# A fused transformer block: order of the LayerNorm statistics, choice of the tile transposed ahead of K, and the PSUM banks that go with them

## Chip, cores, metric

One core of one Trainium2 chip. The metric is device time in microseconds of one execution. The kernel before took 245.29 us (median of 3; 245.23 to 245.52). A program on one core has no sister core to compare with; by the rule used here a run more than 1.5% above the fastest of its kernel is slow.

## The reference, cut to what matters

```python
B, N, D = 2, 256, 1152          # 512 tokens: tiles 0,1 are batch 0, tiles 2,3 batch 1
mod = (_silu(c) @ w_mod).reshape(B, 6, 1, D)
shift_a, scale_a, gate_a, shift_m, scale_m, gate_m = [mod[:, i] for i in range(6)]
h = _layernorm(x) * (1 + scale_a) + shift_a
qkv = (h @ wqkv)...             # then attention, @ wo, a second LayerNorm, fc1, gelu, fc2
```

This is about the first 14 us: the first LayerNorm, the columns of `1 + scale_a`, and the start of the K projection.

## The kernel before

Every operation is a unit with its reads and writes; a scheduler orders the units (PE in program order, the head of VectorE by a list) and derives the waits. It tracks PSUM by bank and orders any two engines that touch one bank, one after the other (in the trace of before ScalarE's hk_2_0 starts at 12.13 us, VectorE's hk_1_0 on the same bank has ended at 12.09).

```python
for t in range(4):                       # statistics of LN1
    if t in (1, 2): ln_stats_dve(...)    # VectorE: 3 bn_stats (L743), aggregate (L744), + eps (L746); GpSimd: pow -0.5 (L747)
    else:           ln_stats_act(...)    # ScalarE: sum (L751), sum of squares (L753); then var (L754), GpSimd pow (L755)
    dve(... (x - m) * rs ..., "xn_%d" % t)                                   # L764

XB = [(4, 5, 3), (6, 5, 7)]              # PSUM banks of the transposed tiles, by batch
KB = [(0, 1, 2, 3), (4, 5, 6)]           # PSUM banks of K's accumulators, by batch
...                                      # warm(n): n matmuls 128x512 whose result nobody reads
xn_T(1)                                  # 9 transposes of tile 1 (L695)
warm(1, "c"); sca(0, 3)                  # 12 matmuls 128x2 for the scale columns; 1st w_mod load
xn_T(0)
warm(1, "d"); sca(3, 6)                  # 2nd w_mod load
warm(1, "e"); sca(6, 9)                  # 3rd w_mod load
hk(0, 0)                                 # VectorE: scale k-tile 0 of batch 0 (L809), reads the scales in PSUM
...                                      # ScalarE copies tiles 0 and 1 out of banks 5 and 3 (L687)
xn_T(3, 0, 8)                            # 8 transposes of tile 3
k_first(0); k_first(1)                   # K, k-tiles 0 and 1, batch 0: 16 matmuls 128x256
xn_T(3, 8, 9); xn_T(2)
```

## Time and profile before

| | before |
|---|---|
| time, median | 245.29 us |
| span of the profiled run | 243.3 us |
| PE busy | 98% |
| x first used (VectorE's first statistics) | 4.78 us |
| K's first 128x256 matmul | 11.78 us |
| last VectorE instruction (L1273) | starts 241.06 us |

### The profile page before, as it was taken

What the parts mean: (1) busy time and instruction counts of PE and PEld (TensorE: products, weight loads), DVE (VectorE), ACT (ScalarE), POOL (GpSimd) and SP (SyncE); (2) the same over time, 40 slices, a digit from 0 to 9 for tenths busy, and PEclk for the clock granted to TensorE, in tenths of its full rate; (3) what the DMA queues carried; (4) which work ended last, traced back from release to release, by engine and by line L of the source; (5) the groups of instructions that cost most, each with busy time, mean ns of one, the idle gap of its engine ahead of it and who ended that gap; (6) DMA issues with size and microseconds to landing.
All of it is one profiled execution on the core that took longest, in us unless ns stands there. A gap on an engine that the chain in (4) does not pass through costs nothing.

```text
span 243.3 us, 4087 instructions
## 1 busy us (share of the span) xinstructions
PE 238.9 (98%) x1763; PEld 148.1 (61%) x1763; DVE 120.4 (49%) x217; ACT 67.2 (28%) x136; POOL 21.4 (9%) x39
## 2 busy tenths in 40 slices
PE   7999999999999999999999999999999999999995
PEld 2698854556667666898444444444565666656575
DVE  3824378596997799789999500000022221111112
ACT  4830350345424207973233222223000000000000
POOL 1500000000021186400000000020000000000000
PEclk9999999999999999999999999999999999999999
DMA  7999999999995999989953498002000000000000
GB/s 233 332 379 393 390 390 391 396 414 405 392 354 183 341 396 392 392 268 394 316 160 84 150 320 310 0 21 80 0 16 19 16 16 19 16 16 22 29 16 19
DMA packets 30140, 51.59 MB, mean 212 GB/s; under 512 B 1703, under 2 KB 15787, under 8 KB 30123
## 3 DMA queue, kind: packets, MB, share of 16 engines
q1 hardware_dynamic: 29680, 50.14, 57.9%
q0 software_dynamic: 416, 1.19, 1.7%
q8 instruction: 14, 0.23, 0.4%
q14 instruction: 3, 0.02, 0.0%
q10 hardware_dynamic: 27, 0.00, 0.0%
HBM read 50.14 MB, written 1.19 MB: 211 GB/s over the span
## 4 chain that ended last, share of the span: by engine, by line
PE 94%; ACT 2%; DMA 2%; DVE 1%; POOL 0%; issue 0%; DVEq 0%
PE psum L692 93%; PE psum L695 2%; DMA arena<-in_x_dram 2%; ACT arena L753 1%; ACT arena L751 1%; DVE arena L764 0%; POOL arena L755 0%; DVE arena L1272 0%; DVE arena L1273 0%; DVE arena L754 0%; DVE arena L746 0%; DVEq L476 0%
## 5 line engine op out<-in xcount | busy, mean ns | idle before, releaser
L692 PE MATMUL psum<-arena 128*128 128x384 bf16 (+10 forms) x1674 | 235.7, 307 | 1.5 <-POOL arena L715 1.5
L692 PEld LDWEIGHTS psum<-arena 128*128 128x128 bf16 (+3 forms) x1674 | 142.9, 97 | 90.1 <-issue 4.5
L1067 DVE SCALAR_TENSOR_TENSOR arena<-arena 128x1152 f32<-128x1152 bf16 x32 | 44.7, 1414 | 0.6
L1272 DVE TENSOR_TENSOR arena<-psum,arena 128x384 f32<-128x384 f32 (+3 forms) x14 | 7.0, 501 | 68.0 <-PE psum L692 68.0
L1181 ACT ACTIVATE arena<-psum 128x512 bf16<-128x512 f32 (+1 forms) x44 | 22.4, 520 | 42.7 <-PE psum L692 42.7
L687 ACT ACTIVATE arena<-psum 128x512 bf16<-128x512 f32 (+6 forms) x37 | 19.6, 550 | 38.7 <-PE psum L692 37.0
L689 DVE CAST arena<-psum 128x512 bf16<-128x512 f32 (+3 forms) x13 | 8.2, 641 | 11.4 <-PE psum L692 11.3
L673 POOL DMA_DIRECT2D dit_scratch<-arena x3 | 1.8, 616 | 115.3 <-DVE arena L689 58.5
L1149 POOL TENSOR_TENSOR arena<-arena 128x384 f32<-128x384 f32 x12 | 10.9, 912 | 10.8 <-DVE arena L1148 9.4
L1094 DVE CAST arena<-psum 72x32 bf16<-72x32 f32 x1 | 0.2, 188 | 21.3 <-PE psum L692 21.3
L743 DVE BATCH_NORM_STATS2 arena<-arena 128x6 f32<-128x384 f32 (+1 forms) x18 | 9.6, 551 | 0.3
L1154 ACT ACTIVATE arena<-arena 128x1152 bf16<-128x1152 f32 x4 | 5.3, 1344 | 11.8 <-DVE arena L1153 11.8
L1273 DVE TENSOR_TENSOR arena<-arena 128x384 bf16<-128x384 f32 (+3 forms) x14 | 7.0, 501 | 0.5
L1148 DVE TENSOR_TENSOR arena<-psum,arena 128x384 f32<-128x384 f32 x12 | 6.5, 547 | 1.5 <-PE psum L692 1.4
L695 PE MATMUL psum<-arena 128*128 128x128 bf16 (+1 forms) x89 | 7.1, 219 | 0.2 <-DVE arena L764 0.2
L695 PEld LDWEIGHTS psum<-arena 128*128 128x128 bf16 (+1 forms) x89 | 5.8, 98 | 2.2 <-DMA arena<-in_c_dram 0.8
L1168 DVE TENSOR_SCALAR arena<-psum,arena 128x128 bf16<-128x128 bf16 x20 | 5.4, 334 | 1.9 <-PE psum L695 1.9
L1171 ACT ACTIVATE arena<-psum,arena 128x128 bf16<-128x128 bf16 x16 | 6.0, 456 | 1.0 <-PE psum L692 0.6
L1074 DVE TENSOR_REDUCE arena<-arena 128x36 f32<-128x1152 f32 x4 | 5.4, 1345 | 0.0
L1071 DVE STREAM_TRANSPOSE arena<-arena 128x1152 f32<-128x1152 f32 x4 | 5.4, 1362 | 0.0
L997 ACT ACTIVATE arena<-psum,arena 128x256 bf16<-128x256 f32 x8 | 3.7, 472 | 1.3 <-PE psum L692 0.9
L951 ACT ACTIVATE arena<-arena 128x256 bf16<-128x256 bf16 x6 | 2.6, 498 | 3.9 <-DVE arena L945 3.9
(48 smaller groups left out, 45.9 us busy)
## 6 DMA issues: line engine op xcount, KB each, us to landing
arena<-in_w_fc_dram SPq DMA_DIRECT2D x9, 1152.0 KB, 7.1
arena<-in_w_fc_dram SPq DMA_DIRECT2D x4, 2592.0 KB, 17.3
arena<-in_wqkv_dram SPq DMA_DIRECT2D x18, 288.0 KB, 10.4
arena<-in_w_mod_dram SPq DMA_DIRECT2D x3, 1728.0 KB, 20.3
arena<-in_w_mod_dram SPq DMA_DIRECT2D x3, 864.0 KB, 13.4
arena<-in_w_mod_dram SPq DMA_DIRECT2D x9, 288.0 KB, 10.7
arena<-in_wqkv_dram SPq DMA_DIRECT2D x1, 2592.0 KB, 16.7
arena<-in_wo_dram SPq DMA_DIRECT2D x1, 2592.0 KB, 24.4
```

Of the source, the lines that this page charges most:

```text
L687: act(c_act(n), lambda e: e.activation(out=dst, in_=src, func=ACTF.Copy), [src], [dst], name)
L689: dve(c_dve_psum16(n) if psum16 else c_dve_psum32(n), lambda e: e.tensor_copy(dst, src), [src], [dst], name)
L692: S.instr(lambda e: e.matmul(o, lhsT=l, rhs=r, start=st, stop=sp, **kw), reads=[l, r], writes=[o])
L695: S.instr(lambda e: e.transpose(o, i_, idn), reads=[i_, idn], writes=[o])
L743: dve(550, lambda e, s=s, o=o: e.bn_stats(out=o, in_=s), [s], [o], "bn_%s_%d" % (tag, ci))
L1067: dve(1270, lambda e, w=w, s=s, acc=acc: e.scalar_tensor_tensor(out=acc, in0=w, scalar=s, in1=acc, op0=ALU.mult, op1=ALU.add), [w, s, acc] ...
L1148: dve(550, lambda e, o=o, ga=ga, x1c=x1c: e.tensor_tensor(out=x1c, in0=o, in1=ga, op=ALU.mult), [o, ga], [x1c], "wo_t1_%d_%d" % (t, ci))
L1149: S.op("pool", 930, lambda e, xs=xs, x1c=x1c: e.tensor_tensor(out=x1c, in0=x1c, in1=xs, op=ALU.add), reads=[x1c, xs], writes=[x1c], name=" ...
L1171: act(440, lambda e, o=o, dst=dst, s1=s1, s2=s2: e.activation(out=dst, in_=o, func=ACTF.Identity, scale=s1, bias=s2), [o, s1, s2], [dst], ...
L1181: act(c_act(ntok), lambda e: e.activation(out=dst, in_=o, func=ACTF.Gelu_apprx_tanh), [o], [dst], "gelu_%d_%d" % (f, tok0))
L1272: dve(c_dve_psum32(w), lambda e, o=o, gm=gm, t1=t1: e.tensor_tensor(out=t1, in0=o, in1=gm, op=ALU.mult), [o, gm], [t1], "fc2_t1_%d_%d" % ( ...
L1273: dve(c_dve_32(w), lambda e, t1=t1, x1c=x1c, ost=ost: e.tensor_tensor(out=ost, in0=t1, in1=x1c, op=ALU.add), [t1, x1c], [ost], "fc2_out_%d ...
```

## The change

Its intent: the tile whose transposes stand ahead of K shall be one that does not wait for ScalarE's four passes over x. So tile 2 takes tile 3's place, its statistics run without xn_0 between them, tile 0 is transposed later, and banks are renamed so that tile 2's transposes and K find free ones.

```diff
-XB = [(4, 5, 3), (6, 5, 7)]
+XB = [(4, 5, 3), (6, 2, 7)]
-KB = [(0, 1, 2, 3), (4, 5, 6)]
+KB = [(0, 1, 5, 3), (4, 2, 6)]
 sca(0, 3)
-xn_T(0)
 warm(1, "d")
 sca(3, 6)
+xn_T(0)
...
-xn_T(3, 0, 8)
+xn_T(2, 0, 8)
...
-xn_T(3, 8, 9)
-xn_T(2)
+xn_T(2, 8, 9)
+xn_T(3)
 # VectorE's list
-"xn_1", "bn_ln1_2_1", "xn_0", "bn_ln1_2_2", "aggr_ln1_2", "var_ln1_3", "veps_ln1_2", "xn_3", "hk_0_0", ..., "xn_2"
+"xn_1", "bn_ln1_2_1", "bn_ln1_2_2", "aggr_ln1_2", "veps_ln1_2", "xn_0", "var_ln1_3", "xn_2", "hk_0_0", ..., "xn_3"
 # GpSimd
-S.order_after(by["rstd_ln1_2"], by["rstd_ln1_3"])
+S.order_after(by["rstd_ln1_3"], by["rstd_ln1_2"])
```

More of the change, by code (lines that the diff above doesn't have):

```diff
@@ L960, in build_kernel @@
             "dve": ["zq4b", "c_half", "c_silu", "bn_ln1_1_0", "bn_ln1_1_1", "bn_ln1_1_2", "aggr_ln1_1", "veps_ln1_1", "bn_ln1_2_0",
-                    "xn_1", "bn_ln1_2_1", "xn_0", "bn_ln1_2_2", "aggr_ln1_2", "var_ln1_3", "veps_ln1_2", "xn_3", "hk_0_0", "sc1a_0", "hk_1_0",
-                    "xn_2", "hk_0_1", "hk_1_1", "hk_2_1", "hk_3_1", "hk_%d_0" % KC, "sc1a_4", "hk_%d_1" % KC] + ["hk_%d_%d" % (kt, b) for kt in range(KC + 1, KT) for b in range(2)],
+                    "xn_1", "bn_ln1_2_1", "bn_ln1_2_2", "aggr_ln1_2", "veps_ln1_2", "xn_0", "var_ln1_3", "xn_2", "hk_0_0", "sc1a_0", "hk_1_0",
+                    "xn_3", "hk_0_1", "hk_1_1", "hk_2_1", "hk_3_1", "hk_%d_0" % KC, "sc1a_4", "hk_%d_1" % KC] + ["hk_%d_%d" % (kt, b) for kt in range(KC + 1, KT) for b in range(2)],
             "act": ["ld_c", "c_tanh", "sum_ln1_0", "sq_ln1_0", "sum_ln1_3", "sq_ln1_3", "xnT_cp0_4", "xnT_cp0_8", "hk_2_0", "hk_3_0",
```

## The prediction

K's start moves from 11.78 to 11.59 us, a gain of 0.19, shaded to 0.18, and 245.29 - 0.18 gives 245.11. "16 such matmuls" are K's 128x256 ones, and "serialises them by bank" speaks of two engines at one bank.

> **What bounds the kernel now.** I read the page first: busy shares, then the chain that ended last, then the costliest groups.
>
> ```profile
> span 243.3 us, 4087 instructions
> PE 238.9 (98%) x1763; PEld 148.1 (61%) x1763; DVE 120.4 (49%) x217; ACT 67.2 (28%) x136; POOL 21.4 (9%) x39
> PE 94%; ACT 2%; DMA 2%; DVE 1%; POOL 0%; issue 0%; DVEq 0%
> L692 PE MATMUL psum<-arena 128*128 128x384 bf16 (+10 forms) x1674 | 235.7, 307 | 1.5 <-POOL arena L715 1.5
> L695 PE MATMUL psum<-arena 128*128 128x128 bf16 (+1 forms) x89 | 7.1, 219 | 0.2 <-DVE arena L764 0.2
> ```
>
> TensorE (PE) holds 94% of the chain and stands idle for 1.5 us at the start and 0.2 us once later. The remaining 6% of the chain, some 14 us, is the head, and the chain in order of time shows it (columns: start, length, what).
>
> ```profile
> 8.50 1.26 ACT arena L753 x2
> ...
> 9.86 0.16 DVE arena L754
> 10.02 0.07 DVE arena L746
> ...
> 10.10 0.56 POOL arena L755
> 10.66 0.03 issue
> 10.69 0.59 DVE arena L764
> 11.28 0.05 issue
> 11.32 0.62 PE psum L695 x8
> 11.94 1.75 PE psum L692 x16
> 13.69 0.56 PE psum L695 x10
> 14.25 45.14 PE psum L692 x382
> ```
>
> Up to 11.32 us the chain is the LayerNorm of token tile 3: ScalarE sums its squares (L753), VectorE makes the variance (L754), GpSimd 1/sqrt (L755), VectorE normalises (L764), and PE transposes it. From 11.32 on nothing but PE is in the chain until the final eviction. So a change in the head is worth exactly the time by which PE's unbroken stream starts earlier, provided no new gap appears behind it. PE is called busy before 11.32 too, but much of that is warm-up matmuls whose result nobody reads, and a few real ones.
>
> The timeline of the last two microseconds before that stream shows who else stands close behind (start, length, engine, line, operation).
>
> ```profile
> 8.44 0.58 DVE L764 TENSOR_SCALAR arena<-arena 128x1152 bf16<-128x1152 bf16 x1
> 8.94 0.55 DVE L743 BATCH_NORM_STATS2 arena<-arena 128x6 f32<-128x384 bf16 x1
> 9.52 0.23 DVE L744 BATCH_NORM_AGGREGATE arena<-arena 128x2 f32<-128x18 f32 x1
> 10.00 1.30 ACT L687 ACTIVATE arena<-psum 128x1024 bf16<-128x1024 bf16 x2 [0.24 <-PE psum L695]
> 10.62 0.68 POOL L747 TENSOR_TENSOR arena<-arena 128x1 f32<-128x1 f32 x1
> 10.68 0.38 PEld L692 LDWEIGHTS psum<-arena 128*128 128x128 bf16 x12 [0.28 <-DMA arena<-in_w_mod_dram]
> 11.28 0.35 DVE L809 TENSOR_SCALAR arena<-psum 128x256 bf16<-128x256 bf16 x1
> 11.32 0.45 PEld L695 LDWEIGHTS psum<-arena 128*128 128x128 bf16 x8 [0.26 <-DVE arena L764]
> ```
>
> The line to see is 10.68: the last twelve scale matmuls (`sca(6,9)`) waited 0.28 us for the third load of w_mod. They end at about 11.15 by the trace. So the removed wait (xn_3 at 11.28) has a second limiter only some 0.2 us ahead of it.
>
> [...] `k_first(0)` and `k_first(1)`, 16 such matmuls, run from 11.78 to 13.53, 109 ns each. [...] I expect no clock effect. [...] The kernel serialises them by bank, and the trace agrees: ScalarE's hk_2_0 starts at 12.13, just after VectorE's hk_1_0 on the same bank ends at 12.09. That is why the diff renames banks. [...]
>
> **The change part by part.** No instruction is added or removed; the order changes on PE, VectorE and GpSimd only. All times are estimates from the durations above.
>
> VectorE: the second and third stats pieces of tile 2 run back to back (7.91, then 8.40 at the 0.49 us spacing that tile 1's three showed: 1.48/3), to 8.95. Aggregate 8.98 to 9.22, add epsilon 9.25 to 9.40, then xn_0 at 9.32 to 9.90 instead of 8.44 to 9.02: 0.88 us later. The small variance operation of tile 3 follows at about 9.86 to 10.02. GpSimd takes tile 2's 1/sqrt at 9.43, some 0.57 us, to 10.00. xn_2 then runs from 10.05 to 10.63. Tile 2 is therefore ready 0.65 us before tile 3 was (11.27).
>
> PE: `xn_T(0)` now stands behind `sca(3,6)` and starts at 9.95 when xn_0 is done. Its nine transposes issue at 56 ns each (0.5 us) and the warm-up matmul behind it takes 0.22, so `sca(6,9)` may issue at 10.67. The w_mod load lets it go at 10.68 anyway. Moving tile 0's transposes thus costs nothing, narrowly. The twelve weights load in 0.38, so the eight transposes of tile 2 start at about 11.08 instead of 11.32, without a wait: 0.24 us gained at this point.
>
> Not all of it reaches K. The first K matmul also needs hk_0_0, which reads the scales just made in PSUM, so it starts when `sca(6,9)` ends: 11.15 + 0.04 = 11.19, and with its 0.35 us it ends at 11.54; PE goes on at 11.59. Before, K started at 11.78 (the 0.46 us of eight transposes after 11.32, with hk_0_0 ready at 11.63). Gain: 11.78 - 11.59 = 0.19 us. Three more conditions fit below that. wk0's load was issued at 3.69 and landed 7.7 us later, 11.39. ScalarE's two copies of tiles 0 and 1 out of banks 5 and 3 (1.30 us in all) start when tile 0's transposes end, about 10.65, and end at 11.95 with the first at about 11.55; the third K pair, now in bank 5, wants it at 11.59 + 4 x 0.109 = 12.03, and the fourth, bank 3, at 12.25. hk_1_0 ends near 12.00, wanted at 12.46.
>
> Behind the second k-tile come the last transpose of tile 2 and tile 3's nine, at about 13.33. xn_3 runs where xn_2 ran, about 12.0 to 12.6, so its late statistics do not matter. Everything later keeps its order and moves up by 0.19.
>
> **The rivals.** First, *the new limiter eats it all*: if xn_0 ends 0.2 us later than I add up, or the w_mod load lands later, `sca(6,9)` and hk_0_0 slip and the gain is 0 (245.3). For it: the slack at 10.68 is 0.01 by my sum. Against: each term is a duration from this trace. Second, *the bank moves bite*: bank 5 is now used at once after ScalarE's copy, where before bank 2 had been only warmed up. If the copies slip past 12.03 or 12.25, K stalls 0.1 to 0.3 us and the time is 245.3 to 245.4. The two margins are 0.48 and 0.30 us. Third, *a load takes the place*: wk0 has 0.2 us of slack, wk1 (4.23 + 7.9 = 12.13) 0.3 us, wk4 (8.62 + about 10.7 = 19.3) about 1 us before its use near 20.4. If the DMA stream were a little later in some runs, the gain is halved (245.2). Fourth, *no limiter at 11.15*: if the scales are done sooner than modelled, all 0.24 us survives (245.05).
>
> **Range and chances.** 245.29 - 0.18 (the 0.19 shaded a little for the rivals, which mostly take away) gives 245.11. The three runs of before span 0.29 us, more than the effect, so the range is set by noise and the rivals: 244.85 to 245.4. Two per cent is 4.9 us; the whole head has no such amount to give, since even deleting everything from the end of the x load (4.76) to 11.32 would be 6.6. Faster or slower by 2% gets one chance in a hundred or less.
>
> **What would show it.** Right: VectorE's L764 for tile 0 starts near 9.3, for tile 2 near 10.05; PE's load wait on w_mod is still there at 10.7; tile 2's transposes start near 11.1 with no wait for L764; the first 256-column matmul near 11.6; in the chain, w_mod or L692 stands where L753 to L764 stood. Wrong: a wait of PE for L764 at `xn_T(0)` that pushes `sca(6,9)` past 10.9, a wait for ScalarE's L687 in the first eight K matmuls, or any PE idle time after 14 us that was not there.

## The result

| | before | changed |
|---|---|---|
| time, median (6 runs each) | 245.33 us (245.23 to 245.52) | 245.19 us (244.80 to 245.73) |
| ratio | | 0.9995, 95% interval 0.9982 to 1.0008 |
| span of the profiled run | 243.3 us | 243.3 us |
| x first used | 4.78 us | 4.67 us |
| K's first matmul | 11.78 us | 11.57 us |
| last VectorE instruction | 241.06 us | 240.87 us |

Ratios here are the mean time of one kernel's fast runs over that of the other's of the same rounds, so not quite the ratio of the medians.

245.19 lies beside the predicted 245.11. The trace is sharper than the clock. The chain that ended last, changed kernel, in order of time (start, length, what):

```profile
9.11 0.15 DVE arena L746
9.27 0.50 DVE arena L764
9.81 0.68 PE psum L695 x9
10.54 0.46 PE psum L692 x12
11.00 0.16 PE psum L695 x3
11.16 0.36 DVE arena L809
11.57 1.92 PE psum L692 x16
...
240.87 0.22 DVE arena L1273
```

ScalarE's L753 and tile 3's L764 are gone from it. In their place stand tile 2's statistics and xn_0 on VectorE, tile 0's nine transposes, the twelve scale matmuls and hk_0_0 (L809). K starts 0.21 us earlier and the last VectorE instruction 0.19 us earlier. The spans are equal all the same, because the last store, issued at 241.40 before and 241.20 after, took 1.4 us to land before and 1.6 us after: the end of the kernel has a scatter as large as the gain.

The timeline of the changed kernel, lines between 9 and 11.5 us (start, length, engine, line, operation, and in brackets the idle time ahead of it and who ended it):

```profile
9.18 0.57 DVE L764 TENSOR_SCALAR arena<-arena 128x1152 bf16<-128x1152 bf16 x1
9.35 0.81 POOL L747 TENSOR_TENSOR arena<-arena 128x1 f32<-128x1 f32 x1 [0.63 <-DVE arena L746]
10.20 0.58 DVE L764 TENSOR_SCALAR arena<-arena 128x1152 bf16<-128x1152 bf16 x1 [0.29 <-POOL arena L747]
10.27 0.64 PEld L692 LDWEIGHTS psum<-arena 128*128 128x128 bf16 x13
11.15 0.36 DVE L809 TENSOR_SCALAR arena<-psum 128x256 bf16<-128x256 bf16 x1 [0.38 <-PE psum L695]
```

Three things differ from the forecast. GpSimd's 1/sqrt of tile 2 took 0.81 us, not 0.57; it ran beside xn_0. PE did not wait for the third w_mod load: the line at 10.27, the last warm-up matmul's weights and the twelve of `sca(6,9)`, has no idle time ahead of it (the load, issued at 2.87, landed 7.3 us later, at about 10.2). And x itself arrived 0.11 us earlier in this run. From x's first use, K starts 7.00 us later before and 6.90 us later after: only 0.10 of the 0.21 us can be laid to the change. Whether even that is real needed more traces.

### The profile page after: what moved, and what is told of

Same layout as the page of the kernel before. It is cut to its first block, busy times and chain, and to the rows that moved or that the text cites. A ratio compares the mean times of both kernels' runs of the same rounds, so it can differ in the third digit from the quotient of the medians.

```text
span 243.3 us, 4077 instructions
## 1 busy us (share of the span) xinstructions
PE 238.0 (98%) x1753; PEld 147.7 (61%) x1763; DVE 120.3 (49%) x217; ACT 67.2 (28%) x136; POOL 21.4 (9%) x39
## 4 chain that ended last, share of the span: by engine, by line
PE 95%; DVE 2%; issue 1%; POOL 0%; ACT 0%; DVEq 0%; POOLq 0%
PE psum L692 94%; PE psum L695 2%; DVE arena L743 1%; DVE arena L764 0%; POOL arena L747 0%; DVE arena L744 0%; DVE arena L809 0%; DVE arena L746 0%; POOL arena L715 0%; DVE arena L1272 0%; DVE arena L1273 0%; POOL arena L714 0%; ACT arena L730 0%; DVE arena L731 0%; DVE arena L736 0%
## 5 line engine op out<-in xcount | busy, mean ns | idle before, releaser
L692 PE MATMUL psum<-arena 128*128 128x384 bf16 (+12 forms) x1664 | 234.3, 306 | 2.3 <-POOL arena L715 1.5
L689 DVE CAST arena<-psum 128x512 bf16<-128x512 f32 (+3 forms) x13 | 8.2, 641 | 11.4 <-PE psum L692 11.3
L747 POOL TENSOR_TENSOR arena<-arena 128x1 f32<-128x1 f32 x6 | 3.6, 598 | 1.9 <-DVE arena L746 1.9
## 6 DMA issues: line engine op xcount, KB each, us to landing
arena<-in_w_mod_dram SPq DMA_DIRECT2D x9, 288.0 KB, 10.7
```

The costliest lines, as they stand in the source:

```text
L689: dve(c_dve_psum16(n) if psum16 else c_dve_psum32(n), lambda e: e.tensor_copy(dst, src), [src], [dst], name)
L692: S.instr(lambda e: e.matmul(o, lhsT=l, rhs=r, start=st, stop=sp, **kw), reads=[l, r], writes=[o])
```

## The experiments

All twelve runs in one table. "x" is VectorE's first statistics instruction, "K" the first 128x256 matmul, "end" the start of the last VectorE instruction; all are read from each run's own trace.

| run | x | K | K - x | end - K | what held K | ratio to before, 95% |
|---|---|---|---|---|---|---|
| before, first trace | 4.78 | 11.78 | 7.00 | 229.28 | tile 3's chain | |
| changed, first trace | 4.67 | 11.57 | 6.90 | 229.30 | xn_0, PE, hk_0_0 | 0.9995 (0.9982 to 1.0008) |
| e1 changed again | 4.75 | 11.65 | 6.90 | 229.29 | the same | 0.9998 (0.9985 to 1.0010) |
| e2 before again | 4.58 | 11.59 | 7.01 | 229.30 | tile 3's chain | 1.0002 (0.9990 to 1.0015) |
| e3 swap alone | 4.58 | 11.86 | 7.28 | 229.30 | PE's backlog | 1.0000 (0.9986 to 1.0014) |
| e4 statistics alone | 4.83 | 11.93 | 7.10 | 229.30 | 3rd w_mod load | 0.9999 (0.9987 to 1.0012) |
| e5 no warm-up "e" | 4.69 | 11.69 | 7.00 | 229.31 | 3rd w_mod load | 0.9998 (0.9985 to 1.0010) |
| e6 old banks | 4.57 | 11.72 | 7.15 | 229.29 | ScalarE's copy, and the load | 1.0007 (0.9993 to 1.0021) |
| e7 delay | 4.84 | 14.89 | 10.05 | 230.95 | the delay, slow clock | 1.0164 (1.0140 to 1.0188) |
| e8 no chain from x | 4.90 | 11.87 | 6.97 | 229.29 | 3rd w_mod load | 0.9999 (0.9984 to 1.0015) |
| e9 swap alone again | 4.82 | 11.81 | 6.99 | 229.30 | 3rd w_mod load | 0.9996 (0.9979 to 1.0013) |
| e10 delay, PE kept busy | 4.80 | 14.08 | 9.28 | 229.30 | the delay | 1.0082 (1.0067 to 1.0097) |
| e11 e5 without the load's wait | 4.57 | 11.30 | 6.73 | 229.60 | xn_0, PE | 0.9988 (0.9973 to 1.0003) |
| e12 swap alone, without the load's wait | 4.83 | 11.75 | 6.92 | 229.29 | xn_2 | 1.0000 (0.9983 to 1.0017) |

e8, e11 and e12 compute wrong results; all others were correct.

**e1: the changed kernel again** (no edit), **and e2: the kernel before again** (no edit).

> The changed kernel once more, for a second trace and a narrower interval. In the first pair of traces K's first 256-column matmul moved from 11.78 to 11.57 us, but x was in use at 4.78 before and at 4.67 after, so from x's arrival K starts at 7.00 before and 6.90 after. Theory A (VectorE and PE are now the chain, x to K is fixed): 6.90 +- 0.03 after x is first used, time 0.1 to 0.2 us under before, ratio 0.9992 to 0.9996. Rival N (only scatter of the loads): K at 7.0 after x, ratio 1.000.

> The kernel before against itself: the noise of the method, and a second trace of the head. Theory A: K's first matmul at 7.00 +- 0.03 us after x is first used, because ScalarE's four passes over x (L751, L753) hold the chain; ratio 1.000 within 0.0008. Rival N: K's start after x scatters by 0.1 us or more with the loads, here as well, which would make the 0.10 us between the two first traces worthless.

Both came out at the named values, 6.90 and 7.01. x's arrival scatters by 0.33 us over all traces, the distance from x to K hardly at all where the chain from x holds it. So in these traces the 0.10 us is real, and rival N falls. The time cannot show it: before against itself gave 1.0002 with an interval of 0.0013 to each side, some 0.3 us.

Two more things differ between these four traces. PE's granted clock (the share of its full clock that it is given; before the release the warm-up matmuls take 0.43 us each, after it 0.22) was released late in both traces of before, at 7.07 and 7.12 us by the clock record in the packed traces, and early in both of the changed kernel, at 5.07 and 5.47. That does not make the 0.10 us: in both traces of before PE still stood waiting for tile 3's L764, 0.26 us at 11.32 and 0.19 us at 11.12, though in e2 the scale matmuls behind PE's late queue would have let K start only 0.01 us later than that. And both traces of the changed kernel had an early third w_mod load (landed at 10.18 and 10.53, PE at `sca(6,9)` at 10.54 and 10.62). In e4, e5, e6, e8 and e9 below, this load let PE go only 5.96 to 6.11 us after x. With the 1.01 us found there from `sca(6,9)` to K, the changed kernel would then start K at x + 6.97 at best, and gain 0.03 us or nothing (an estimate from these numbers). So 0.10 us is what the change earns when the load comes early.

**e3: only the swap of the tiles** (new banks, tile 2's 1/sqrt first; the statistics and tile 0's transposes where they were before).

```diff
 # against the kernel before
+XB, KB and the rstd order as in the change
-xn_T(3, 0, 8) ... xn_T(3, 8, 9); xn_T(2)
+xn_T(2, 0, 8) ... xn_T(2, 8, 9); xn_T(3)
-"xn_1", "bn_2_1", "xn_0", "bn_2_2", "aggr_2", "var_3", "veps_2", "xn_3"
+"xn_1", "bn_2_1", "xn_0", "bn_2_2", "aggr_2", "veps_2", "var_3", "xn_2"
```

> Only the swap of tiles 2 and 3 (with the new banks and tile 2's 1/sqrt first); the statistics of tile 2 stay interleaved with xn_0, and tile 0 is transposed where it was before. Theory A1 (the gain comes from no longer waiting for ScalarE's sums): tile 2's epsilon ends near 9.9 us, 1/sqrt near 10.55, xn_2 at 11.15, K at about 11.62, 6.85 to 6.90 us after x, so most or all of the gain without moving the statistics. Rival A2 (the gain needs the statistics ahead): K at 7.0 us after x or later, no gain. Times are expected 0 to 0.2 us under before.

K came at x + 7.28. That is within what rival A2 said (7.0 or later), but not for A2's reason. The reason is in the weight loads of PE (each line a group; the spacing of single ones is the time of one warm-up matmul). e3:

```profile
6.86 0.15 PEld L692 LDWEIGHTS psum<-arena 128*128 128x128 bf16 x1 [0.27 <-issue]
7.29 0.15 PEld L692 LDWEIGHTS psum<-arena 128*128 128x128 bf16 x1 [0.28 <-DVE arena L743]
7.69 0.53 PEld L692 LDWEIGHTS psum<-arena 128*128 128x128 bf16 x3 [0.25 <-issue]
8.34 0.70 PEld L695 LDWEIGHTS psum<-arena 128*128 128x128 bf16 x9
```

and the changed kernel's first trace:

```profile
4.72 0.15 PEld L692 LDWEIGHTS psum<-arena 128*128 128x128 bf16 x1 [0.28 <-issue]
5.12 0.75 PEld L692 LDWEIGHTS psum<-arena 128*128 128x128 bf16 x4 [0.24 <-issue]
7.93 0.51 PEld L695 LDWEIGHTS psum<-arena 128*128 128x128 bf16 x9 [0.50 <-DVE arena L764]
```

In e3 the warm-up matmuls followed each other at 0.43 us until 7.7 us, and tile 1's transposes came out of the queue late and without a wait; in the other trace the pace quickened at about 5.1 us, and PE then waited half a microsecond for xn_1. 0.43 us is twice the 0.22 us that the same matmuls take after the quickening, and over the fourteen traces the quickening came between 4.64 us (e7) and 7.65 us (e3) by their clock records (4.69 and 7.69 by their weight loads). The clock column of the views does not show it: it has 1.00 from 5 to 7 us in e3, where the matmuls still took 0.43 us. A late release is read from their spacing. So PE's own backlog is another possible limiter of K, in either kernel, and e3 tells nothing about the swap.

**e4: only the statistics ahead** (and tile 0's transposes later; new banks; tile 3 stays ahead of K).

```diff
 # against the kernel before
+XB, KB as in the change
 sca(0, 3)
-xn_T(0)
 warm(1, "d"); sca(3, 6)
+xn_T(0)
-"bn_2_1", "xn_0", "bn_2_2", "aggr_2", "var_3", "veps_2", "xn_3"
+"bn_2_1", "bn_2_2", "aggr_2", "veps_2", "xn_0", "var_3", "xn_3"
```

> Only the statistics of tile 2 ahead of xn_0, and tile 0 transposed behind the second group of scale matmuls (with the new banks); tile 3 is still the one ahead of K. Theory A1: tile 3's variance still waits for ScalarE, which ends near 9.76 us (4.98 after x), so xn_3 ends near 11.2 and K starts 7.0 us after x: no gain. Rival A2: K at 6.90 after x. Times 0 to 0.1 us from before.

No gain, as theory A1 had it; but K came 0.10 us later still than tile 3's chain would allow. The weight loads of e4 say why:

```profile
10.92 0.38 PEld L692 LDWEIGHTS psum<-arena 128*128 128x128 bf16 x12 [0.39 <-DMA arena<-in_w_mod_dram]
```

The third w_mod load came late, and K followed 1.01 us after it: 11.93. This 1.01 is the same in e5, e8 and e9 (10.68 to 11.69, 10.86 to 11.87, 10.80 to 11.81).

**e5: the changed kernel without the warm-up matmul ahead of sca(6,9).**

```diff
-warm(1, "e")
 sca(6, 9)
```

> The changed kernel without the one warm-up matmul between tile 0's transposes and the last scale matmuls sca(6,9). Theory A (three limiters for K's first matmul, the latest wins: the chain from x, 6.90 us in the changed kernel; the third w_mod load, landing + 1.05; PE's own backlog when its clock was released late): the chain from x shortens by the matmul's 0.22 us, so K at x + 6.68, unless the load lands later than x + 5.6, which then shows as a wait of PE for w_mod. Rival: the warm-up matmul was hidden, K stays at x + 6.90. Time 0 to 0.3 us under before; too small for the interval.

Not x + 6.68 but x + 7.00. The exception written into the expectation is what happened. e5's timeline:

```profile
10.68 0.38 PEld L692 LDWEIGHTS psum<-arena 128*128 128x128 bf16 x12 [0.29 <-DMA arena<-in_w_mod_dram]
11.28 0.36 DVE L809 TENSOR_SCALAR arena<-psum 128x256 bf16<-128x256 bf16 x1 [0.48 <-PE psum L695]
11.69 0.55 PEld L692 LDWEIGHTS psum<-arena 128*128 128x128 bf16 x6 [0.24 <-DVE arena L809]
```

PE was ready and waited for the load; hk_0_0 began 0.60 us after the scale matmuls did, and K 0.41 us after that.

**e6: the changed orders with the old banks.**

```diff
-XB = [(4, 5, 3), (6, 2, 7)]
+XB = [(4, 5, 3), (6, 5, 7)]
-KB = [(0, 1, 5, 3), (4, 2, 6)]
+KB = [(0, 1, 2, 3), (4, 5, 6)]
```

> The changed orders with the old PSUM banks (tile 2's transposes 4 to 7 in bank 5, which still holds tile 0 and 1's transposes). Theory A: they wait until ScalarE has copied bank 5, which ends 6.8 us after x is first used; PE shows a wait of some 0.3 us for ScalarE (L687) in the middle of the eight transposes, and K starts at x + 7.05 to 7.10: the whole gain is gone. Rival: the bank names do not matter, K at x + 6.90. Time equal to before within 0.2 us.

The wait for ScalarE's copy of bank 5 is there, in the middle of tile 2's transposes:

```profile
11.49 0.23 PEld L695 LDWEIGHTS psum<-arena 128*128 128x128 bf16 x4 [0.26 <-ACT arena L687]
```

K came at x + 7.15 (expected 7.05 to 7.10). In this run the load too was late (PE released at 10.68, so 11.69 by the 1.01 rule), so the banks cost only 0.03 us beyond it. But the copy starts when tile 0's transposes end, x + 5.84 here, whatever the load does, so with the old banks K could not have come before x + 7.15 even with an early load. So without the renaming the new order starts K later than the old one did (7.15 against 7.00 after x, one trace). The renaming alone was not run.

**e7: the changed kernel with four extra passes of statistics over a piece of tile 2.**

```diff
 if tag == "ln1_2":
+    for r in range(4): bn_stats of the third piece again, into the same place
 dve(... bn_aggr ...)
```

> The changed kernel with four more passes of statistics over one piece of tile 2 (0.49 us each by their spacing, results unchanged) ahead of its aggregation: the step that the change shortened, lengthened by 1.96 us. Theory A (nothing behind the head has any slack, all traces so far have 229.30 us from K's first matmul to the last VectorE instruction): K at x + 8.86, 229.30 us kept, time + 1.96 against the changed kernel and + 1.86 against before, ratio 1.0076. Rival 1: the loads, which go on during the delay, let the later stages catch up: less than 1.5 us arrive at the end. Rival 2: PE's 2 us of idling slow its clock for a while: more than 2.3 us arrive.

Rival 2 came true. The passes took 2.34 us in all, 0.59 us each instead of 0.49 (why was not tested), K came 3.15 us later than the undelayed 6.90, and from K to the end it took 230.95 us instead of 229.30. e7's windows, each with the span of the window, then busy time (instructions) of PE, PE's weight loads, VectorE, ScalarE, GpSimd, then PE's granted clock, the DMA share and GB/s:

```profile
11.00:12.00 1.00, 0.00 (x0) 0.00 (x0) 0.93 (x4) 0.00 (x0) 0.10 (x1) 0.73 1.04 401
12.00:13.00 1.00, 0.64 (x7) 0.65 (x8) 0.63 (x3) 0.00 (x0) 1.00 (x2) 0.50 1.05 396
17.00:18.00 1.00, 1.00 (x7) 0.73 (x5) 0.00 (x0) 0.00 (x0) 0.00 (x0) 0.50 1.04 387
18.00:19.00 1.00, 1.00 (x15) 0.86 (x14) 0.00 (x0) 0.00 (x0) 0.00 (x0) 0.85 1.11 404
```

PE had nothing to do from 9.83 to 12.36 us; its clock fell to half at about 11.5 (0.73 in that window), 1.6 us into this gap, and rose again at about 18.3, 5.9 us after PE resumed. Half clock from K's start at 14.89 to 18.3 costs 1.7 us (an estimate from these two times), which is the stretch seen behind K (1.65 us); ahead of K the half clock cost 0.77 us more, as e10 shows below (10.05 against 9.28). The profiled run was the slowest of its four (250.16 us, the others 248.61 to 249.03), and the clock says why: its mean granted clock was 0.986, that of the others 0.993, so by an estimate from these means they spent some 3.5 us at half clock and it 6.8. So the medians, not its span, give the size: 3.87 us above before.

**e8: all tiles normalised with tile 1's mean and 1/sqrt**, so that none ahead of K needs statistics of its own (wrong).

```diff
-m = MV[:, t, 0:1]
+m, rs = MV[:, 1, 0:1], RSTD[:, 1:2]
-sca(0, 3); warm(1, "d"); sca(3, 6); xn_T(0)
+sca(0, 3); xn_T(0); warm(1, "d"); sca(3, 6)
-"xn_1", "bn_2_1", "bn_2_2", "aggr_2", "veps_2", "xn_0", "var_3", "xn_2"
+"xn_1", "xn_0", "xn_2", "bn_2_1", "bn_2_2", "aggr_2", "veps_2", "var_3"
```

> Wrong results on purpose: all four tiles are normalised with tile 1's mean and 1/sqrt, so the tiles ahead of K need no statistics of their own and are ready by about x + 4.4; tile 0 is transposed where it was before. All other instructions still run. It shows what is left when the whole chain from x is out of the way. Theory A: the third w_mod load takes over: K at its landing + 1.05, about 11.2 to 11.7 us after the start, so at most 0.3 us more than the change gained; in a run where PE's clock is released late (after 7 us), PE's backlog holds K at 11.5 or later. Rival: K starts below 11.0, so the load was not the next limit.

K came at 11.87 us (expected at most 11.7) with PE released by the w_mod load at 10.86. With the whole chain from x out of the way the head is no shorter: the third w_mod load is the next limit, and it stands right behind.

**e9: e3 again** (no new edit), for a run without the backlog.

> The swap alone a second time, because in its first trace PE's clock was released late (its 512-column warm-up matmuls took 0.43 us until 7.7 us) and PE's backlog, not a wait, set K's start at x + 7.28. Theory A1: in a run with the clock released by 7.2 us, xn_2 ends at x + 6.40 as in the first trace and K starts at the later of x + 6.90 and the start of sca(6,9) + 1.01, so the statistics moved ahead add nothing. Rival A2: K at x + 7.0 or later although neither w_mod nor the backlog holds it. The time stays within 0.2 us of before.

K at 10.80 + 1.01 = 11.81, by the load. xn_2 had ended at 11.23; PE transposed it from 11.29, and 0.46 us for the eight transposes would have let K start at 11.75, only 0.06 us earlier.

**e10: e7 with PE kept busy.**

```diff
 sca(3, 6)
+warm(9, "x")
 xn_T(0)
```

> e7 again, with nine warm-up matmuls of 0.22 us (1.95 us in all) ahead of tile 0's transposes, so that PE is not idle during the delay. Theory C (in e7 the clock fell to half after PE had idled, which cost 1.65 us more than the delay): the clock stays at 1.00, the four passes cost 2.34 us as in e7, K at x + 9.24, and 229.30 us from K to the last VectorE instruction: time + 2.3 against before, 1.6 us less than e7. Rival: the late stages, not the clock, stretched e7: then 230.9 us from K to the end here too.

K at x + 9.28 (expected 9.24), 229.30 us from there to the last VectorE instruction, and no fall of the clock after its release at 7.53 us (1.00 in every window from 9 to 19 us). K's first matmul and the wait ahead of it:

```profile
14.08 0.99 PEld L692 LDWEIGHTS psum<-arena 128*128 128x128 bf16 x10 [0.27 <-DVE arena L812]
```

(L812 is hk_0_0 in this kernel.) In this run, with the clock at 1.00, the delay in the head arrives at the end one for one; the rival for e7 falls. The time rose by 0.0082 of 245.3, 2.0 us; K moved by 2.30 against the first trace of before, which the interval (1.6 to 2.4 us) contains. By the medians over before of the same rounds, e7 lost 3.87 us and e10 1.96.

**e11: e5 with sca(6,9) reading the second w_mod load's rows** (wrong), so that the third cannot hold it.

```diff
-mod_kt(WSC, kt, 0, "sca_%d" % kt, (0, KC))
+mod_kt(WSC, kt, 0, "sca_%d" % kt, (0, KC), kt - 3 if kt > 5 else kt)   # last argument: k-tile of W
```

> e5 (no warm-up matmul ahead of sca(6,9)) with sca(6,9) reading the rows of the second w_mod load in place of the third, so that it need not wait for the third load, which is still done: results wrong on purpose. Theory A (in e5 the third load took over): sca(6,9) follows tile 0's transposes at once and K starts at x + 6.68 or when wk0 has landed (11.0 to 11.5 us after the start), unless PE's backlog holds it. Rival (the load was not what held e5): K at x + 6.90 to 7.0 as there. The time moves by 0.2 us at most.

K at x + 6.73, 11.30 us: the load was what held e5. But here, for the only time among the runs at full clock, the distance to the end grew, to 229.60. PE still led the first changed trace by 0.27 us at 92.97 (its 93.245), then waited at the start of fc1 for VectorE's L1167, the eviction of tile 1's second-LayerNorm transposes. One of three such lines:

```profile
98.46 0.10 PEld L692 LDWEIGHTS psum<-arena 128*128 128x128 bf16 x1 [0.16 <-DVE arena L1167]
```

In this run the first eviction of the output projection was at 83.79 us, no earlier than the 83.67 of that trace, although PE was ahead. In e5 the trace names the load of the attention gate as what that eviction waited for; in e11 itself it names PE. So the second LayerNorm may be tied to that load rather than to PE, and a head some 0.3 us shorter would then gain nothing more. That is read from one trace and not tested.

**e12: e3 without the load's wait** (the same edit as e11, on e3; wrong).

> The swap alone (as e3, e9) with sca(6,9) reading the second w_mod load's rows, so that the third load can't hold K: results wrong on purpose. In e9 xn_2 ended at x + 6.41; 0.05 to PE and 0.46 for eight transposes put K at x + 6.92 if nothing else holds it. Theory A1: K at x + 6.90 to 6.95 against 6.90 for the whole change, so the statistics moved ahead are worth 0.05 us or less and the swap is the gain. Rival A2: K at x + 7.0, so the swap alone gives nothing. If PE's clock is released after 7.5 us the run can't tell, since PE's backlog then sets K.

Here nothing else interferes:

```profile
11.30 0.62 PE L695 MATMUL psum<-arena 128*128 128x128 bf16 x8 [0.45 <-DVE arena L764]
11.75 0.71 PE L692 MATMUL psum<-arena 128*128 128x256 bf16 x5
```

PE waits for xn_2 and K starts at x + 6.92, as expected to the hundredth. The swap gives 0.08 of the change's 0.10 us; the statistics moved ahead and tile 0's later transposes give 0.02, and in e4 nothing alone. That is one trace, and 0.02 is hardly more than the 0.01 between the two traces of before.

No version beat both kernels clear of noise. e11's arrangement was nearest, and it is wrong.

## Why the prediction was right

**The bound.** Right: from K to the last VectorE instruction it takes 229.28 to 229.31 us in eleven of fourteen traces whose K starts range from 11.57 to 11.93, and 229.30 after e10's long delay. Only e7 (clock) and e11 (a new wait near 98 us) differ. The "some 14 us" of chain outside PE are not all head, though: 11.3 us are, and some 2.5 us are the tail.

**VectorE's and PE's order.** Right but for one sign. Shifted by the 0.11 us by which x came earlier, xn_0 runs 9.29 to 9.86 (forecast 9.32 to 9.90) and `sca(6,9)` starts at 10.65 (forecast 10.68). But the forecast's "PE's load wait on w_mod is still there at 10.7" did not come in either changed trace: the chain through xn_0 and tile 0's transposes set the pace, not the load.

**The 1/sqrt on GpSimd.** Off by 0.24 us, 0.81 instead of 0.57, without effect: xn_2 was still done (10.78) before PE came to it (10.86). The forecast took the shortest value; its own view shows this L747 at 0.68 beside xn_3. The traces agree on a pattern: the 1/sqrt takes 0.55 to 0.57 us with no normalisation running, and where it starts with 0.25, 0.38 or 0.40 us of one still to run (before, e3, changed), 0.66, 0.79 and 0.81, so it ends 0.41 us after the normalisation (e8, with three in a row, aside). What lengthens it was not shown: GpSimd's L754 took only 0.19 us wholly beside xn_1 (before, 7.47 to 7.66), and no run was made to test it. The longer 1/sqrt leaves 0.08 us of margin where the forecast counted on 0.45.

**The size, 0.19 us.** This is the mis-sized sum: it is 0.10 us from x to K (e1, e2). That K came 0.21 us earlier in the first pair of traces, beside the forecast's 0.19, is luck: 0.11 of it is x. The term that failed is "it starts when `sca(6,9)` ends: 11.15 + 0.04 = 11.19". From the start of the twelve matmuls to hk_0_0 the forecast thus allowed 0.51 us; it takes 0.60 (e5) to 0.61 (changed). VectorE began to read the result 0.15 us after the end that the trace models for a 2-column matmul (11.00 to 11.15), where the forecast took 0.04, the distance that the trace of before shows behind a 128-column transpose (14.25 to 14.29).

**The rivals.** The first, that the new limiter eats the gain, was the best of them: the third w_mod load held K in e4, e5, e8 and e9, and in e6 all but 0.03 us of it, and by the 1.01 us it would have let K of the first trace start at 11.69 at best, 0.09 us before the 11.78 seen. The second was right in its mechanism only for the old banks (e6). wk0 and wk1 never held K. The fourth, that all of 0.24 us survives, fell. The forecast did not see PE's backlog behind a late clock release (e3) as a limiter; it said only that it expected no clock effect of the change, which holds (in the changed kernel's first trace the granted clock is 1.00 from 5.07 us to the end of the span). One of its grounds was misread, though: the clock row of before is 9 in all 40 slices because the page counts the time before the first clock event as full; the record begins at 7.07 us, and the warm-up matmuls took 0.43 us each until then.

**Range and chances.** Right, and for the reason given: the head had little to give, and noise is larger than what it gave. In the two sets of runs the changed kernel's ratio was 0.9995 and 0.9998. That the median 245.19 lies beside 245.11 is no evidence for the mechanism: the five sets of before have medians from 245.08 to 245.38.

## What to carry to other kernels

Before taking a wait out of a head, write down when each of the others would let the same matmul start: here the statistics, one weight load and PE's own warm-up queue all came within 0.3 us, so removing the slowest was worth 0.1 us. When an effect is smaller than the scatter of the time, measure distances inside the trace between two events of the same run (x to K, K to end) rather than times from the start. And filler matmuls were not free decoration here: without them (e7 against e10) a gap of 2.5 us cost 1.9 us more by the medians, and 2.4 us more in the profiled run.
